# Top-32 attention and capacity routing: which engine makes the product and the mask of a unit, and when a pair is turned

## The chip, the cores and the metric

The kernel runs on one core of a Trainium2 chip. A core has five engines that work side by side, each with its own queue of instructions in order: TensorE (PE in the profile, its weight loads PEld), VectorE (DVE), ScalarE (ACT), GpSimd (POOL) and SyncE (SP), which issues the DMA here. The metric is the device time of one execution in microseconds (us), the median of several runs.

## The reference

Attention of 8 batches x 8 heads over 576 tokens, head dimension 64, in which every row keeps only its 32 largest scores; its output goes into a routed layer with 8 experts of 80 tokens each.

```python
scores = scale * np.matmul(q, k.transpose(0, 1, 3, 2))       # q, k, v: (8, 8, 576, 64), float32
kth = np.partition(scores, -32, axis=-1)[..., -32:-31]
scores = np.where(scores >= kth, scores, -1000000000.0)
attn = np.exp(scores - np.max(scores, axis=-1, keepdims=True))
attn = attn / (np.sum(attn, axis=-1, keepdims=True) + 1e-09)
x = np.matmul(attn, v)                  # then (B,H,S,D) -> (4608, 512)
# ... gate: softmax of x @ w_gate, the best expert of each token
# ... each expert keeps its 80 tokens of highest gate weight:
#     out = gate_w * (relu(x @ w1) @ w2), zero for all other tokens
```

The change touches the attention only.

## The kernel before

Two heads of one batch make a head pair (32 of them). A pair's 576 rows are cut into four tiles of 128 rows and a tail of 64. A **unit** is one tile of one head, 128 rows of 576 scores; the tails of both heads make one unit together. So a pair has 9 units, and there are 288.

A unit's way: TensorE multiplies q and k (`front`), ScalarE copies the scores to SBUF (`s`). VectorE finds candidates for the largest (`parts`, six pieces of 96), and `search` takes the 24th largest of them as a guess. ScalarE compares all scores with the guess and counts (`sign`, with an accumulated `cnt`). The **product** `y` of scores and signs leaves the scores below the guess with their order, so that one more maximum gives the eight next ones; the **pick** takes out of these, by the count, the exact 32nd largest, `thr`. The **mask** marks what lies below it.

```python
        def search(self, i):
            # ... three maxima of the candidates, with two match_replace between; after the third:
                    sign = self.rows.tile([P, S], BF16, name="sign", tag="sign")
                    cnt = self.small.tile([P, 1], F32, name="cnt", tag="cnt")
                    nc.scalar.activation(sign, s, Act.Sign, bias=w9[:, 7:8], scale=-1.0, accum_out=cnt)
                yield
            # ...
            y = self.rows.tile([P, S], F32, name="y", tag="y", bufs=1)
            engine = nc.gpsimd if i in self.odd else nc.vector
            engine.tensor_tensor(out=y, in0=s, in1=sign, op=Alu.mult)
            yield
            nc.vector.max(out=w9[:, 8:], in_=y)
            yield
            pick = self.small.tile([P, TOP_K - G0 + 1], F32, name="pick", tag="pick")
            nc.vector.scalar_tensor_tensor(out=pick, in0=past, scalar=cnt, in1=w9[:, 7:], accum_out=self.thr[:, i : i + 1],
                                           op0=Alu.is_equal, op1=Alu.mult)
            yield
```

The product is made by GpSimd for the units in `odd`, by VectorE for the others. The mask is made by ScalarE for the units in `odd`, by GpSimd for the others:

```python
        def below(self, i):

            self.top.pop(i)
            mask = self.mask_of(i)
            if i in self.odd:
                nc.scalar.activation(mask, self.s[i], Act.Relu, bias=self.thr[:, i : i + 1], scale=-1.0)
                return
            nc.gpsimd.tensor_scalar(mask, self.s[i], self.thr[:, i : i + 1], None, op0=Alu.is_lt)
```

`turn_w` **turns** the scores of a whole tile (both heads) on TensorE and adds the turned mask, times a very large negative number, into the same PSUM. ScalarE takes the exponential out of PSUM (`wT`). `back` multiplies with v, `over` takes the reciprocal of the row sums, `divide` scales the output, and `norm` stores it, turns it (`xT`) and multiplies with the gate's weights (logits).

```python
        def turn_w(self, n, t, between=None):
            # ...
            for c, o in enumerate(dst):
                nc.tensor.matmul(o, lhsT=sc[:, keys[c]], rhs=ident, start=c in (0, NF, NF + 1), stop=False, is_transpose=True,
                                 skip_group_check=True)
            if between:
                between()

            for c in sorted(range(len(dst)), key=lambda c: c != NF):
                nc.tensor.matmul(dst[c], lhsT=mk[:, keys[c]], rhs=minus if self.lean else huge, start=False, stop=True,
                                 skip_group_check=True)
            # ... two exponentials on ScalarE
```

`front`, `turn` (q and k of the next pair), the turn in `norm` and the logits share one PSUM tile with a single buffer, `self.ps_s`.

A whole tile's or the tail's last unit is `whole`. `run` writes out the instructions in steps. Step i works on several units at different stages; the schedule is manual, so each engine gets its instructions in this order. The letters: `G` one of the six candidate maxima of unit i, `a` the first maximum of its candidates, `b c d e` the rest of the search for unit i-1 (`e` ends with ScalarE's sign), `y` the product, `g` the maximum over it, `h` the pick, `m` the mask, `z` the reciprocals.

```python
            self.odd = set(range(1, NU, 2))
                # ...
                lag = dict(a=0, b=1, c=1, d=1, e=1, y=2, g=3, h=4, m=4)

                for c in "ghmGbGycGdGGGeaz" if i % 2 else "GbGhmgcGdGeGGyaz":
                    if c == "G":
                        if 0 <= i < NU:
                            next(first[i])
                    elif c == "a":
                        if 0 <= i < NU:
                            next(first[i], None)
                            second[i] = self.search(i)
                            next(second[i])
                    elif c == "z":
                        for u in drawn:
                            self.over(*u)
                    elif c == "m":
                        if 0 <= i - lag[c] < NU:
                            self.below(i - lag[c])
                    elif i - lag[c] in second:
                        next(second[i - lag[c]])
                done = list(drawn)
                # ...
                def back():
                    if whole(i - 5):
                        self.back(*units[i - 5][:2])
                        drawn.append(units[i - 5][:2])
                # ...
                rest = whole(i - 4) and units[i - 4][2] == 2
                if rest:
                    back()
                def gate():
                    for g in later:
                        if ready[g] == 2:
                            ready[g] = next(g)

                if whole(i - 4):
                    self.turn_w(*units[i - 4][:2], gate)
                for u in done:
                    self.divide(*u)
                # ...
                f = i + 4 if i not in (0, 1) else i + 3
                busy = 0 <= f < NU and units[f][2] != 1
                if busy:
                    self.front(*units[f][:2])
                if not rest:
                    back()
                if due and not busy and i > 0:
                    self.turn(due.pop())
                    busy = True
                for g in list(later):
                    if (ready[g] == 1 and busy or ready[g] == 2 and i < NU + 4) and not last:
                        continue
                    busy = busy or ready[g] == 1
                    ready[g] = next(g, None)
                # ... the next stage of norm
```

Of the kernel before, what the change touches and what calls it, by code (L numbers as in the profile page):

```python
# [9 lines left out]
F32 = mybir.dt.float32  # L10
# [17 lines left out]
def kernel(  # L28
# [12 lines left out]
    B, H, S, D = q.shape  # L41
# [8 lines left out]
    P = 128  # L50
# [13 lines left out]
    NU = NP * UPP  # L64
# [84 lines left out]
    class Attention:  # L149


        def __init__(self, stack, lean):
            self.lean = lean
            pool = lambda name, bufs, **kw: stack.enter_context(tc.tile_pool(name=name, bufs=bufs, **kw))
            self.nat, self.qkp, self.rows = pool("nat", 1), pool("qkp", 2), pool("rows", 2)
            self.small, vpool = pool("small", 4), pool("vpool", 1)
            self.ps_s, self.ps_w, self.ps_c = (pool(n, k, space=PSUM) for n, k in (("ps_s", 1), ("ps_w", 1), ("ps_c", 2)))
            self.qk, self.turned, self.lg = {}, {}, {}
            self.s, self.top, self.cnt, self.y, self.mask, self.w, self.xn = ({} for _ in range(7))
            self.both_s = {}  # L160
            self.thr, self.z = thr_all, z_all
            self.odd = set()


            self.vb = []
            for j in range(1 if lean else 3):
                t = vpool.tile([P, 3 * NF + 4, D + 1], F32, name=f"vb{j}")
                nc.gpsimd.memset(t[:, :, D : D + 1], 1.0)
                nc.gpsimd.memset(t[TL:, 3 * NF, :], 0.0)
                nc.gpsimd.memset(t[:TL, 3 * NF + 1 :, :], 0.0)  # L170
                self.vb.append(t)

            self.xT = vpool.tile([P, NK * P], F32, name="xT")
            nc.gpsimd.memset(self.xT[:, S:], 0.0)
# [49 lines left out]
        def front(self, n, t):  # L224

            qT, kT = self.turned[n]
            m = P if t < NF else TL
            i = n * UPP + 2 * t
            ps = self.four()
            for j in range(2):  # L230
                for h in range(2):
                    d = slice(D * h, D * h + D)
                    o = ps[:, 2 * h + j, :HS] if t < NF else ps[TL * h : TL * h + TL, j, :HS]
                    nc.tensor.matmul(o, lhsT=qT[d, t * P : t * P + m], rhs=kT[d, j * HS : (j + 1) * HS], start=True, stop=True)  # L234
            g = 2 if t < NF else 1
            s = self.rows.tile([P, 2 * S], F32, name="s", tag="s", bufs=2 if self.lean else 5)
            self.both_s[n, t] = s
            for h in range(g):
                self.s[i + h] = s[:, h * S : (h + 1) * S]
            for j in range(0, 2 * g, 2 if i == 0 else 2 * g):  # L240
                w = 2 if i == 0 else 2 * g
                nc.scalar.activation(s[:, j * HS : (j + w) * HS].rearrange("p (j c) -> p j c", c=HS), ps[:, j : j + w, :HS],  # L242
                                     Act.Copy, scale=TINY)
# [205 lines left out]
        def run(self, slow):  # L449

            units = []
            for n in range(NP):
                for t in range(NF):
                    units += [(n, t, 0), (n, t, 1)]
                units.append((n, NF, 2))
            self.odd = set(range(1, NU, 2))
            first, second = {}, {}
            later = []
            due = []
            drawn = []  # L460
            ready = {}

            def whole(i):

                return 0 <= i < NU and units[i][2] > 0

            def step(i, last):
                if 0 <= i < NU:
                    n, t, h = units[i]
                    if t == 2 and h == 1 and n + 2 < NP:  # L470
                        self.load(n + 2, *divmod(n + 2, HP))
                    if t == 3 and h == 1 and n + 2 < NP:
                        self.load_v(n + 2, *divmod(n + 2, HP))
                    if t in (1, 3) and h == 0 and slow and n:
                        slow.pop(0)()
                    if t == 0 and h == 0 and n + 1 < NP:
                        due.append(n + 1)
                    first[i] = self.parts(i)

                lag = dict(a=0, b=1, c=1, d=1, e=1, y=2, g=3, h=4, m=4)  # L480

                for c in "ghmGbGycGdGGGeaz" if i % 2 else "GbGhmgcGdGeGGyaz":
                    if c == "G":
                        if 0 <= i < NU:
                            next(first[i])
# [6 lines that stand above are left out]
                        for u in drawn:  # L492
                            self.over(*u)
                    elif c == "m":
                        if 0 <= i - lag[c] < NU:
                            self.below(i - lag[c])
                    elif i - lag[c] in second:
                        next(second[i - lag[c]])
                done = list(drawn)
                drawn.clear()  # L500

                def back():
                    if whole(i - 5):
                        self.back(*units[i - 5][:2])
                        drawn.append(units[i - 5][:2])


                rest = whole(i - 4) and units[i - 4][2] == 2
                if rest:
                    back()  # L510
                def gate():
                    for g in later:
                        if ready[g] == 2:
                            ready[g] = next(g)

                if whole(i - 4):
                    self.turn_w(*units[i - 4][:2], gate)
                for u in done:
                    self.divide(*u)

                ends = [(n, range(NK) if n < NP - 1 else range(NF) if t < NF else range(NF, NK))
                        for n, t in done if t == NF or (n == NP - 1 and t == NF - 1)]
# [8 lines that stand above are left out]
                    self.turn(due.pop())  # L531
                    busy = True
                for g in list(later):
                    if (ready[g] == 1 and busy or ready[g] == 2 and i < NU + 4) and not last:
                        continue
                    busy = busy or ready[g] == 1
                    ready[g] = next(g, None)
                    if ready[g] is None:
                        later.remove(g)
                for n, cs in ends:  # L540
                    b, hp = divmod(n, HP)
                    later.append(self.norm(n, b, hp, b % 2, 2, cs))
                    ready[later[-1]] = 0

            with tc.manual_schedule():
                for n in range(2):
                    self.load(n, *divmod(n, HP))
                    self.load_v(n, *divmod(n, HP))
                nc.sync.dma_start(wg, moe_w_gate.rearrange("(c p) e -> p c e", p=P))
                self.turn(0)  # L550
                i = -4
                while i < NU + 6 or later:
                    step(i, i >= NU + 5)
                    i += 1
            assert not slow and not due

# [389 lines left out]
```

## Time and profile before

989.52 us, median of 3 runs (988.08 to 991.57). The profiled execution has a span of 986.1 us.

| engine | busy us | share of the span |
|---|---|---|
| TensorE | 865.1 | 88% |
| VectorE | 866.3 | 88% |
| ScalarE | 786.7 | 80% |
| GpSimd | 451.9 | 46% |

The attention takes the span up to about 860 us; routing and experts follow. Shares of the whole span mix both, so the stretches of the attention are to be read by themselves. A row of the groups names the line of the kernel, the engine, the operation, what is written and read, the shape, the count, the busy time in us, the mean duration in ns of one, and behind the bar the time that the engine sat idle before these instructions, with what ended most of it. Instructions of one engine overlap a little at their ends, so busy time is less than the sum of the durations. In the list of waits each line gives the engine that waited, for what, the total in us, the number of times and the longest.

### The profile page before, as it was taken

The page shows a single profiled execution, that of the slowest core. Times are in us where ns is not written, and L with a number is a line of the kernel's source. Part 1 is how long each engine was busy: PE and PEld are TensorE (multiplying, and loading weights), DVE is VectorE, ACT ScalarE, POOL GpSimd, SP SyncE. Part 2 cuts the span into 40 slices and gives each one's busy share as a digit, 9 for nine tenths or more (in the row PEclk, how much of TensorE's full clock was granted, in tenths as well). Part 3 has the DMA queues.
Part 4 walks back from the last instruction along what each step waited for, and adds up shares of the span by engine and source line. Part 5 has one row for each costly group of instructions (what it writes and reads, how often), then busy time and mean ns, then how long its engine had stood idle before and what let it go on. Part 6 is the DMA issues. An engine that isn't in the chain of part 4 may idle for free.

```text
span 986.1 us, 35265 instructions
## 1 busy us (share of the span) xinstructions
PE 865.1 (88%) x13112; PEld 679.3 (69%) x13112; DVE 866.3 (88%) x5072; ACT 786.7 (80%) x1652; POOL 451.9 (46%) x333
## 2 busy tenths in 40 slices
PE   5898989898898998998889898988898898699896
PEld 3676767676666776776667676666676776578896
DVE  5999999999999999999999999999999999561110
ACT  4899999999899999999999999998999998501110
POOL 2455545555455555454555555554555555201111
PEclk9999999999999999999999999999999999979999
DMA  3445453333333333332221222222222200085910
GB/s 86 111 131 139 133 141 100 100 99 99 80 95 99 88 93 99 99 99 68 57 57 48 52 50 53 57 57 57 57 57 56 55 17 14 17 338 180 375 52 25
DMA packets 189812, 90.99 MB, mean 92 GB/s; under 512 B 139712, under 2 KB 176576, under 8 KB 189632
## 3 DMA queue, kind: packets, MB, share of 16 engines
q1 hardware_dynamic: 188608, 86.03, 31.5%
q0 software_dynamic: 1024, 2.62, 0.9%
q8 instruction: 105, 1.72, 0.7%
q14 instruction: 75, 0.61, 0.2%
HBM read 68.44 MB, written 20.19 MB: 90 GB/s over the span
## 4 chain that ended last, share of the span: by engine, by line
DVE 59%; PE 29%; ACT 7%; issue 3%; POOL 1%; DMA 1%; SPq 0%; POOLq 0%; ACTq 0%; DVEq 0%
DVE cand L250 19%; DVE w L275 14%; DVE cand L269 7%; DVE y L273 7%; PE cc L357 6%; PE sp L234 4%; DVE top L261 4%; PE yp L830 4%; PE sp L209 4%; DVE pick L278 3%; DVE w L261 2%; PE ab L334 2%; ACT wT L344 2%; ACT mask L294 1%; PE ab L340 1%
## 5 line engine op out<-in xcount | busy, mean ns | idle before, releaser
L250 DVE MAX8 cand<-s 128x8 f32<-128x96 f32 x1728 | 389.6, 246 | 9.1 <-ACT s L242 8.9
L296 POOL TENSOR_SCALAR mask<-s,thr_all 128x576 bf16<-128x576 f32 x144 | 247.9, 1722 | 149.6 <-DVE pick L278 130.1
L273 POOL TENSOR_TENSOR y<-s,sign 128x576 f32<-128x576 f32 x144 | 184.5, 1281 | 261.8 <-DVE pick L278 121.9
L266 ACT ACTIVATE sign<-s,w 128x576 bf16<-128x576 f32 x288 | 224.9, 781 | 29.6 <-DVE w L261 27.3
L357 PEld LDWEIGHTS cc<-vb,wT 128*64 128x64 f32 x5760 | 182.1, 138 | 92.0 <-ACT wT L344 90.7
L357 PE MATMUL cc<-vb,wT 128*64 128x65 f32 x5760 | 204.4, 225 | 25.7 <-ACT wT L344 25.7
L275 DVE MAX8 w<-y 128x8 f32<-128x576 f32 x288 | 216.6, 752 | 1.3 <-POOL y L273 1.3
L234 PE MATMUL sp<-both 64*128 64x288 f32 (+1 forms) x1280 | 202.0, 435 | 5.7 <-ACT s L242 3.8
L242 ACT ACTIVATE s<-sp 128x1152 f32<-128x1152 f32 (+1 forms) x161 | 167.6, 1042 | 10.5 <-PE sp L234 9.8
L334 PE MATMUL ab<-ident,s 128*128 128x128 f32 x1148 | 175.9, 281 | 0.0
L344 ACT ACTIVATE wT<-ab 128x1024 f32<-128x1024 f32 (+1 forms) x159 | 149.6, 941 | 5.6 <-PE ab L340 4.1
L234 PEld LDWEIGHTS sp<-both 64*128 64x128 f32 (+1 forms) x1280 | 105.5, 179 | 45.2 <-ACT s L242 6.2
L334 PEld LDWEIGHTS ab<-ident,s 128*128 128x128 f32 x1148 | 127.2, 141 | 11.7 <-issue 0.9
L340 PEld LDWEIGHTS <-mask 128*128 128x128 bf16 x1312 | 76.9, 97 | 79.1 <-issue 37.3
L261 DVE MAX8 top<-cand 128x8 f32<-128x48 f32 x576 | 115.2, 200 | 0.0
L294 ACT ACTIVATE mask<-s,thr_all 128x576 bf16<-128x576 f32 x144 | 113.0, 785 | 0.5
L269 DVE MATCH_REPLACE8 cand<-top,cand 128x48 f32<-128x48 f32 x576 | 111.0, 193 | 0.1
L273 DVE TENSOR_TENSOR y<-s,sign 128x576 f32<-128x576 f32 x144 | 106.6, 740 | 0.8 <-ACT sign L266 0.8
L340 PE MATMUL ab<-huge,mask 128*128 128x128 bf16 x1148 | 89.9, 219 | 0.0
L340 PE MATMUL cc<-huge,mask 128*128 128x128 bf16 x160 | 35.7, 223 | 58.9 <-ACT mask L294 29.0
L380 ACT ACTIVATE xn<-cc,z_all 128x64 f32<-128x64 f32 (+1 forms) x320 | 85.8, 315 | 1.2 <-DVE z_all L369 0.8
L278 DVE SCALAR_TENSOR_TENSOR pick<-past,cnt,w 128x9 f32<-128x9 f32 x288 | 66.4, 230 | 0.2 <-DVE z_all L369 0.2
(187 smaller groups left out, 856.0 us busy)
## 6 DMA issues: line engine op xcount, KB each, us to landing
w<-in_moe_w_dram SPq DMA_DIRECT2D x10, 2048.0 KB, 16.0
vb<-in_v_dram SPq DMA_DIRECT2D x96, 128.0 KB, 2.7
w<-in_moe_w_dram SPq DMA_DIRECT2D x24, 512.0 KB, 3.8
out_dram<-zero SPq DMA_DIRECT2D x9, 1024.0 KB, 5.8
qn<-in_q_dram SPq DMA_DIRECT2D x64, 128.0 KB, 2.3
kn<-in_k_dram SPq DMA_DIRECT2D x64, 128.0 KB, 2.6
xd<-xn SPq DMA_DIRECT2D x32, 256.0 KB, 2.2
qn<-in_q_dram SPq DMA_DIRECT2D x32, 32.0 KB, 2.5
```

What stands on the lines that cost most here:

```text
L234: nc.tensor.matmul(o, lhsT=qT[d, t * P : t * P + m], rhs=kT[d, j * HS : (j + 1) * HS], start=True, stop=True)
L250: nc.vector.max(out=cand[:, j, :], in_=s[:, j * S // NG : (j + 1) * S // NG])
L261: nc.vector.max(out=dst, in_=cand)
L266: nc.scalar.activation(sign, s, Act.Sign, bias=w9[:, 7:8], scale=-1.0, accum_out=cnt)
L269: nc.vector.match_replace(out=cand, in_to_replace=dst, in_values=cand, imm_value=LOW)
L273: engine.tensor_tensor(out=y, in0=s, in1=sign, op=Alu.mult)
L275: nc.vector.max(out=w9[:, 8:], in_=y)
L296: nc.gpsimd.tensor_scalar(mask, self.s[i], self.thr[:, i : i + 1], None, op0=Alu.is_lt)
L334: nc.tensor.matmul(o, lhsT=sc[:, keys[c]], rhs=ident, start=c in (0, NF, NF + 1), stop=False, is_transpose=True, skip_group_check=True)
L340: nc.tensor.matmul(dst[c], lhsT=mk[:, keys[c]], rhs=minus if self.lean else huge, start=False, stop=True, skip_group_check=True)
L344: nc.scalar.activation(wT[:, : g * NF, :], ab.rearrange("p h c r -> p (h c) r")[:, : g * NF, :], Act.Exp, scale=scale / TINY)
L357: nc.tensor.matmul(cc[r : r + TL, o], lhsT=wT[:, h * NF + c if c < NF else 2 * NF, r : r + TL], rhs=vb[:, k, :], start=(c == 0), stop=(c = ...
```

## The change

The pattern of who makes what goes from every second unit to two of three: of three successive units, two have GpSimd's product and ScalarE's mask, one has VectorE's product and GpSimd's mask. So 192 instead of 144 products are GpSimd's and 96 instead of 144 VectorE's; 192 instead of 144 masks are ScalarE's and 96 instead of 144 GpSimd's. It is meant to take work from VectorE.

VectorE and GpSimd are to be kept out of each other's way: in the step in which VectorE makes a product, the maximum over GpSimd's last product, the pick and the masks stand late, just before VectorE's product; GpSimd's mask comes one step later than before (5 steps behind its unit). So that masks are there before they are needed, a tile is turned 6 instead of 4 steps behind its second unit, and multiplied with v 7 instead of 5 behind. The scores live two steps longer, and get 7 instead of 5 buffers; the small tiles get 5 instead of 4.

```diff
@@ class Attention @@
-            self.small, vpool = pool("small", 4), pool("vpool", 1)
+            self.small, vpool = pool("small", 5), pool("vpool", 1)
 ...
-            s = self.rows.tile([P, 2 * S], F32, name="s", tag="s", bufs=2 if self.lean else 5)
+            s = self.rows.tile([P, 2 * S], F32, name="s", tag="s", bufs=2 if self.lean else 7)
@@ run @@
-            self.odd = set(range(1, NU, 2))
+            self.odd = set(i for i in range(NU) if i % 3 < 2)
 ...
-                lag = dict(a=0, b=1, c=1, d=1, e=1, y=2, g=3, h=4, m=4)
-
-                for c in "ghmGbGycGdGGGeaz" if i % 2 else "GbGhmgcGdGeGGyaz":
+                lag = dict(a=0, b=1, c=1, d=1, e=1, y=2, g=3, h=4)
+
+                for c in "GbGcGdGeGghmGyaz" if i % 3 == 1 else "ghmGbGycGdGGGeaz":
 ...
-                        if 0 <= i - lag[c] < NU:
-                            self.below(i - lag[c])
+
+                        for k in (4, 5):
+                            if 0 <= i - k < NU and (i - k in self.odd) == (k == 4):
+                                self.below(i - k)
 ...
                 def back():
-                    if whole(i - 5):
-                        self.back(*units[i - 5][:2])
-                        drawn.append(units[i - 5][:2])
+                    if whole(i - 7):
+                        self.back(*units[i - 7][:2])
+                        drawn.append(units[i - 7][:2])
 ...
-                rest = whole(i - 4) and units[i - 4][2] == 2
+                rest = whole(i - 6) and units[i - 6][2] == 2
 ...
-                if whole(i - 4):
-                    self.turn_w(*units[i - 4][:2], gate)
+                if whole(i - 6):
+                    self.turn_w(*units[i - 6][:2], gate)
 ... the ends of the loops over the steps are moved by 2 as well
```

More of the change, by code (lines that the diff above doesn't have):

```diff
@@ L533, in step @@
                 for g in list(later):
-                    if (ready[g] == 1 and busy or ready[g] == 2 and i < NU + 4) and not last:
+                    if (ready[g] == 1 and busy or ready[g] == 2 and i < NU + 6) and not last:
                         continue
@@ L551, in run @@
                 i = -4
-                while i < NU + 6 or later:
-                    step(i, i >= NU + 5)
+                while i < NU + 8 or later:
+                    step(i, i >= NU + 7)
                     i += 1
```

## The prediction, made before the changed kernel was run

> **What bounds the kernel now.** I read the page first (engines, slices, groups), then stretches of 100 us, the list of waits, and last the order of time over one cycle of nine units (one head pair). In the stretches (columns: span, then PE, PE weight load, DVE, ACT, POOL busy, granted clock, DMA share, GB/s):
> ```profile
> 300.00:400.00 100.00, 89.69 (x1292) 68.87 (x1292) 99.80 (x599) 93.08 (x197) 52.35 (x35) 1.00 0.35 93
> ...
> 500.00:600.00 100.00, 90.41 (x1305) 69.69 (x1301) 99.91 (x601) 93.35 (x196) 52.32 (x35) 1.00 0.23 55
> ...
> 94.11:770.23 676.12, 606.31 (x8764) 466.90 (x8766) 675.25 (x4046) 627.60 (x1318) 351.29 (x235) 1.00 0.31 79
> ```
> VectorE has no idle time from 100 to 800 us: it is the bound. But ScalarE stands at 93% and TensorE at 90%. GpSimd issues one instruction per unit (a product or a mask), so 94.11 to 770.23 holds 234 units, 26 cycles: 676.12 / 26 = 26.00 us per cycle, and 288 units are 32 cycles. ScalarE's busy time is 627.60 / 26 = 24.14 us of each 26.00.
>
> The groups that the change touches (busy us, mean ns, then the engine's idle time before them):
> ```profile
> L296 POOL TENSOR_SCALAR mask<-s,thr_all 128x576 bf16<-128x576 f32 x144 | 247.9, 1722 | 149.6 <-DVE pick L278 130.1
> L273 POOL TENSOR_TENSOR y<-s,sign 128x576 f32<-128x576 f32 x144 | 184.5, 1281 | 261.8 <-DVE pick L278 121.9
> ...
> L294 ACT ACTIVATE mask<-s,thr_all 128x576 bf16<-128x576 f32 x144 | 113.0, 785 | 0.5
> ...
> L273 DVE TENSOR_TENSOR y<-s,sign 128x576 f32<-128x576 f32 x144 | 106.6, 740 | 0.8 <-ACT sign L266 0.8
> ```
> GpSimd, at 46% of the span, has room; ScalarE has not. The waits that bear on it:
> ```profile
> PEld L340 <- POOL mask L296: 31.1, 21, 1.9
> PE cc L340 <- ACT mask L294: 29.0, 40, 0.8
> ACT sign L266 <- DVE w L261: 27.3, 53, 1.3
> ...
> ACT both L222 <- PE sp L209: 21.7, 31, 2.1
> ```
> TensorE waits for masks of both engines, without cost while VectorE is full. ScalarE's idle time is of two kinds: 27.3 us waiting for VectorE, which goes away when VectorE is no longer the bound, and waits for TensorE, which need not.
>
> **What the Trainium skill says.** "SBUF — State Buffer", section "Who interferes with whom": a VectorE instruction with two SBUF inputs and a GpSimd instruction that reads SBUF exclude one another; whoever comes second waits for the whole of the first. The trace agrees once, near the end:
> ```profile
> 845.85 1.28 POOL L273 TENSOR_TENSOR y<-s,sign 128x576 f32<-128x576 f32 x1 [1.04 <-DVE pick L278]
> 845.87 1.29 DVE L278 SCALAR_TENSOR_TENSOR pick<-past,cnt,w 128x9 f32<-128x9 f32 x1
> ```
> A pick of 213 ns (median) took 1.29 us, just the length of GpSimd's product. In the middle there is hardly a collision: VectorE's products have a mean of 740 ns and a maximum of 759. One that started at 504.95 still took 0.74 us though a GpSimd mask was recorded until 505.22, so the lock's last quarter microsecond is not seen here. "ScalarE: Activation LUTs", section "What ACT_TABLE_LOAD costs", gives an ACTIVATE with a pointer bias 280 ns + 0.833 ns per element, and an overlap of about 93 ns with the next: my estimate for 576 elements is 760 and 667 net; the trace has 785, and 0.67 from a mask's start to the next start (514.54 to 515.21).
>
> **The change part by part.**
>
> *VectorE.* 48 of its 144 products go to GpSimd. From such a product's start to the next instruction's start is 0.66 us (821.94 to 822.60), so 1.5 per cycle free 0.99 us: 26.00 - 0.99 = 25.01 us. If nothing else mattered, 32 x 0.99 = 32 us.
>
> *GpSimd.* 48 products more, 48 masks fewer: 48 x (1.281 - 1.722) = -21 us. It does not bind.
>
> *ScalarE.* 48 masks more, 1.5 x 0.67 = 1.0 us per cycle. The sum of one cycle after, by start-to-next-start times read between 505.82 and 525.99: 9 signs x 0.765 = 6.89; 6 masks x 0.67 = 4.02; exponentials 4 x (0.19 + 0.92) + 0.72 = 5.16; divisions 4 x 0.39 + 0.64 = 2.20; copies of scores 4 x 1.01 + 0.53 = 4.57; turned q and k 1.02; the x turn 0.54; gate part 0.08. Together 24.48 us, half a microsecond under VectorE's 25.01. That is without any wait for TensorE.
>
> *Order.* The new string gives VectorE's product and the pick of that step a place after GpSimd's product and mask. Counting along it, a sign has some 1.5 to 2 us until its product is needed, about as before. A late GpSimd mask can still hold the pick.
>
> *Turn two steps later.* This takes away TensorE's waits for masks (58.9 us in the group of the first mask matmul). But it also puts other work side by side. By position in the cycle, the turns stood at steps 5, 7, 0, 2, 3 and the score matmuls at 5, 7, 0, 2, 4; now both stand at 0, 2, 4, 5, 7. The short tail unit's turn falls at step 5, straight after step 4 with its turn, its gate logits (moved there from step 0) and its scores. And the PSUM tile for scores has one buffer, shared by scores, q/k turns, x turn and logits, so ScalarE and TensorE hand it to and fro.
>
> With ScalarE as the late engine and its signs always ready, I laid that handover out by the trace. From a score copy's end to ScalarE's next use of the same tile:
> 1. x turn, step 3: TensorE needs 1.08 us from the sign's start (505.82 to 506.90) and ScalarE has only a sign of 0.77: idle 0.31.
> 2. q/k turn, step 1: 1.87 us (511.65 to 513.52) against a sign and a mask, 1.45: idle 0.42.
> 3. step 4: the logits between transposes and mask matmuls put the exponentials some 0.1 us late.
> 4. step 5: exponential, value product, tail turn and scores in a row. The same links in the trace:
> ```profile
> 516.16 1.03 ACT L344 ACTIVATE wT<-ab 128x1024 f32<-128x1024 f32 x1
> ...
> 517.24 1.39 PE L357 MATMUL cc<-vb,wT 128*64 128x65 f32 x40
> ...
> 518.55 0.66 PE L334 MATMUL ab<-ident,s 128*128 128x128 f32 x4
> ...
> 519.53 1.19 PE L234 MATMUL sp<-both 64*64 64x288 f32 x8
> ```
> That is 1.08 + 1.31 + 0.98, then 1.24 for full scores and 0.05 to the copy: 4.66 us. Meanwhile ScalarE has 0.92 + 0.39 + 0.53 + 0.67 + 0.77 + 0.72 = 4.00: idle 0.66.
>
> The four gaps are 1.49 us; 24.48 + 1.49 = 25.97 us per cycle, against 26.00 now. So the place of VectorE's bound would be taken by the ScalarE-TensorE handover at nearly the same length.
>
> *The end.* With the turn later, one more pair is unturned when VectorE has finished. At the end pairs follow one another by 4.25 us (846.65 to 850.90). Less the blocked pick (1.29 - 0.21), some 3 us are added.
>
> Sum: 989.5 - 32 x 0.03 + 3 = 992 us.
>
> **The rivals.**
>
> A. *Handover as bound*, as above: 992. For it: ScalarE's 93%, and the wait for the q/k turn already seen in all 31 of them. Against it: gaps 3 and 4 are laid out by hand, and TensorE, which no longer waits for masks, might come earlier to the tail.
>
> B. *Only the unavoidable gaps remain* (1 and 2): 24.48 + 0.73 = 25.21 us, 32 x 0.79 = 25 us saved, 3 given back: 967. For it: the string and the lag look fitted to each other. With VectorE alone as the bound (25.01) it would be 961; I hold that for unlikely, as ScalarE would need 98% occupancy.
>
> C. *The port collides.* In the step before VectorE's product, GpSimd's product is followed at once by its mask (1.28 + 1.72 = 3.0 us). If signs come late from a full ScalarE, the mask runs into the pick, 0.2 to 0.8 us per cycle. By itself VectorE would be at 25.0 + 0.8 = 25.8, still hidden behind A; in series with A's gaps, 32 x 0.5 = 16 us more: about 1008.
>
> **Range and chances.** I weigh A three to one against B: 0.75 x 992 + 0.25 x 967 = 986 us. An error of 0.3 us per cycle in the hand-laid gaps is 10 us; that, and a part of C above, gives 971 to 1002. Over 2% faster means below 969.7, so B or better: 0.17. Over 2% slower means above 1009.3, so C in full: 0.08. Within 2%: 0.75.
>
> **What would show it.** Right: VectorE falls from 99.9% to 96-97% in the middle stretches and its idle time is put down to ScalarE's sign; ScalarE rises to 96% or more, with its idle time before the q/k copy, the x copy and the score copy after the tail turn; TensorE's waits for masks are nearly gone; nine units take about 25.8 us. Wrong towards B: nine units take 25.2 us, and the score copies don't wait. Wrong towards C: picks or VectorE's products with means well over 230 and 740 ns. Wrong altogether if VectorE stays above 99% with a cycle near 25.0.

## The result: slower by 1.5%, and what the profile after shows

The changed kernel takes 1005.16 us against 990.02 us (medians of four runs each): ratio 1.0153, 95% interval 1.0126 to 1.0179. The prediction was 986 us with a range of 971 to 1002, so the result lies outside it, beyond rival A (992). Rival C's figure, 1008, is nearest, but by luck: the collisions of picks and products that it was made of did not come (below).

The stretches of the changed kernel (columns as before: span, PE, PE weight load, DVE, ACT and POOL busy, clock, DMA share, GB/s):

```profile
69.68:810.12 740.44, 651.02 (x9437) 509.86 (x9438) 708.65 (x4312) 696.06 (x1460) 357.65 (x253) 0.99 0.31 79
500.00:600.00 100.00, 89.04 (x1297) 69.79 (x1297) 95.86 (x587) 95.15 (x200) 48.12 (x34) 1.00 0.22 53
```

The first runs from the third to the thirty-first copy of the turned q and k on ScalarE (the q/k copy, one per head pair): 28 cycles of nine units. In the kernel before the same stretch is 727.70 us:

```profile
71.25:798.95 727.70, 652.92 (x9437) 502.83 (x9438) 726.83 (x4354) 675.80 (x1417) 378.33 (x253) 1.00 0.31 80
```

VectorE is no longer full: 96 instead of 99.9%. ScalarE went from 93 to 94%. No engine is saturated.

The groups of the changed kernel that answer to those shown before (busy us and mean ns of one; then the idle us just before them and what ended most of it):

```profile
L273 POOL TENSOR_TENSOR y<-s,sign 128x576 f32<-128x576 f32 x192 | 245.6, 1279 | 445.8 <-DVE pick L278 168.1
...
L296 POOL TENSOR_SCALAR mask<-s,thr_all 128x576 bf16<-128x576 f32 x96 | 165.3, 1722 | 3.1 <-DVE pick L278 3.1
...
L294 ACT ACTIVATE mask<-s,thr_all 128x576 bf16<-128x576 f32 x192 | 149.2, 778 | 0.8
...
L273 DVE TENSOR_TENSOR y<-s,sign 128x576 f32<-128x576 f32 x96 | 72.1, 751 | 28.5 <-ACT sign L266 28.5
...
L278 DVE SCALAR_TENSOR_TENSOR pick<-past,cnt,w 128x9 f32<-128x9 f32 x288 | 61.2, 212 | 0.0
```

The counts are as meant and the mean durations are near those of before (VectorE's product 751 ns against 740, the picks 212 against 230): the products and picks do not collide. But VectorE now sits idle for 28.5 us in front of its own products, waiting for ScalarE's sign. The list of waits of the changed kernel says what ScalarE in turn waits for (who waits, for whom: us in total, times, longest):

```profile
DVE y L273 <- ACT sign L266: 28.5, 58, 0.8
ACT s L242 <- PE sp L234: 27.4, 36, 2.4
...
ACT both L222 <- PE sp L209: 15.7, 31, 2.1
```

ScalarE waits for TensorE, once per cycle in the score copy, once in the q/k copy, and more shortly in the copy of the turned x. The waits of TensorE for masks, which stood in this list before the change (27.8 us for GpSimd's and 24.3 us for ScalarE's between 100 and 800 us), are gone. What stands at the score copy is the chain laid out in the prediction, in order of time (start in us, length in us, engine, line, operation; in brackets the idle time before it and what ended it):

```profile
499.77 0.64 ACT L397 COPY xT<-sp 128x576 f32<-128x576 f32 x1 [0.20 <-PE sp L209]
...
502.20 1.02 ACT L344 ACTIVATE wT<-ab 128x1024 f32<-128x1024 f32 x1
...
503.28 1.39 PE L357 MATMUL cc<-vb,wT 128*64 128x65 f32 x40
...
503.51 0.66 ACT L242 ACTIVATE s<-sp 128x576 f32<-128x576 f32 x1
...
504.60 0.66 PE L334 MATMUL ab<-ident,s 128*128 128x128 f32 x4
...
505.57 1.24 PE L234 MATMUL sp<-both 64*128 64x288 f32 x8
...
506.86 1.13 ACT L242 ACTIVATE s<-sp 128x1152 f32<-128x1152 f32 x1 [0.58 <-PE sp L234]
...
519.86 1.12 ACT L222 COPY both<-sp 128x1152 f32<-128x1152 f32 x1 [0.32 <-PE sp L209]
```

From the exponential (502.20) to the score copy (506.86) it is 4.66 us, as laid out, and ScalarE is idle for 0.58 us before the copy. This longest link is TensorE's own queue rather than the score tile: ScalarE had done with the tile by 504.17, but the scores of 505.57 stand behind the value product and the tail's turn, which follow one another without a pause. Before the x copy and the q/k copy ScalarE is idle for 0.20 and 0.32 us; there TensorE fills the one score tile again only after ScalarE's score copy. No run gives the tile a second buffer, so what the single buffer costs by itself is not shown.

The starts of the q/k copies, one per cycle, divide the loss. Three of the 28 cycles hold the gates of two batches (the softmax of the logits and the choice of the expert, mostly VectorE's work); the other 25 are called plain.

| | before | after | difference |
|---|---|---|---|
| start to the third q/k copy | 71.25 us | 69.68 us | -1.6 us |
| 25 plain cycles | 25.84 us each | 26.09 us each | +6.3 us |
| 3 cycles with gates | 27.23 us each | 29.36 us each | +6.4 us |
| thirty-first copy to the first turn of the routing (861.02, 878.70) | 62.07 us | 68.58 us | +6.5 us |

Together 17.7 us (from unrounded times), nearly the whole difference of the spans, 1004.1 - 986.1 = 18.0.

The granted clock of TensorE (the third figure from the end of a stretch) differs too. In the kernel before it was 1.00 all through the stretch above. In the changed kernel it was about 0.5 for 3.4 us in each of the three cycles with gates and once at the end, as here; a value product then took 2.37 us instead of 1.39:

```profile
489.30:492.70 3.40, 3.40 (x45) 2.95 (x45) 3.40 (x18) 2.75 (x6) 0.88 (x1) 0.51 0.00 0
...
857.86 2.37 PE L357 MATMUL cc<-vb,wT 128*64 128x65 f32 x40 [1.90 <-ACT wT L344]
```

In each of the three cycles it sets in about when TensorE takes up work again after an idle time of 2.82 us, in which it waited for an exponential. What brings the slow clock about is not shown.

### The profile page after: what moved, and what is told of

Read it like the earlier page. It is cut to its first block, busy times and chain, and to the rows that moved or that the text cites. A ratio compares the mean times of both kernels' runs of the same rounds, so it can differ in the third digit from the quotient of the medians.

```text
span 1004.1 us, 35154 instructions
## 1 busy us (share of the span) xinstructions
PE 865.3 (86%) x13112; PEld 689.6 (69%) x13112; DVE 843.1 (84%) x5024; ACT 810.1 (81%) x1700; POOL 428.4 (43%) x333
## 4 chain that ended last, share of the span: by engine, by line
DVE 45%; PE 25%; ACT 23%; issue 4%; POOL 2%; DMA 1%; POOLq 0%; SPq 0%; DVEq 0%; ACTq 0%
DVE cand L250 14%; DVE w L275 10%; ACT sign L266 9%; PE cc L357 5%; DVE cand L269 5%; PE sp L209 5%; DVE y L273 4%; ACT wT L344 4%; PE yp L832 4%; ACT s L242 4%; DVE top L261 3%; ACT mask L294 2%; DVE pick L278 2%; ACT xn L380 2%; PE sp L234 2%
## 5 line engine op out<-in xcount | busy, mean ns | idle before, releaser
L273 POOL TENSOR_TENSOR y<-s,sign 128x576 f32<-128x576 f32 x192 | 245.6, 1279 | 445.8 <-DVE pick L278 168.1
L250 DVE MAX8 cand<-s 128x8 f32<-128x96 f32 x1728 | 395.4, 247 | 8.8 <-ACT s L242 8.8
L357 PEld LDWEIGHTS cc<-vb,wT 128*64 128x64 f32 x5760 | 184.5, 139 | 140.7 <-ACT wT L344 128.7
L357 PE MATMUL cc<-vb,wT 128*64 128x65 f32 x5760 | 206.9, 226 | 70.4 <-ACT wT L344 68.6
L242 ACT ACTIVATE s<-sp 128x1152 f32<-128x1152 f32 (+1 forms) x161 | 166.9, 1038 | 28.2 <-PE sp L234 27.4
L296 POOL TENSOR_SCALAR mask<-s,thr_all 128x576 bf16<-128x576 f32 x96 | 165.3, 1722 | 3.1 <-DVE pick L278 3.1
L294 ACT ACTIVATE mask<-s,thr_all 128x576 bf16<-128x576 f32 x192 | 149.2, 778 | 0.8
L273 DVE TENSOR_TENSOR y<-s,sign 128x576 f32<-128x576 f32 x96 | 72.1, 751 | 28.5 <-ACT sign L266 28.5
L340 PEld LDWEIGHTS <-mask 128*128 128x128 bf16 x1312 | 84.6, 98 | 2.2
L334 PE MATMUL cc<-ident,s 128*128 128x128 f32 x160 | 45.6, 285 | 33.0 <-ACT xn L380 33.0
L278 DVE SCALAR_TENSOR_TENSOR pick<-past,cnt,w 128x9 f32<-128x9 f32 x288 | 61.2, 212 | 0.0
```

The lines of the kernel that those rows point to most:

```text
L250: nc.vector.max(out=cand[:, j, :], in_=s[:, j * S // NG : (j + 1) * S // NG])
L357: nc.tensor.matmul(cc[r : r + TL, o], lhsT=wT[:, h * NF + c if c < NF else 2 * NF, r : r + TL], rhs=vb[:, k, :], start=(c == 0), stop=(c = ...
```

## The experiments

Theory H: in the changed kernel the plain cycle is a chain handed to and fro between ScalarE and TensorE, in part through the one score tile, with VectorE's own 25.0 us below it. Rivals: VectorE and GpSimd shutting each other out, the port of the prediction (P), the later turn by its places alone (L), ScalarE's masks wherever the turn stands (M). A cycle below always means the distance of two q/k copies, read from the trace; times are medians, ratios to the kernel before on the same chip.

**1. The later turn alone.**

```diff
 # kernel before, with
-                if whole(i - 4):
-                    self.turn_w(*units[i - 4][:2], gate)
+                if whole(i - 6):
+                    self.turn_w(*units[i - 6][:2], gate)
 # likewise back at i - 7; score buffers 7, small buffers 5
```

> The kernel before with the later turn alone (turn 6, value product 7 steps behind, 7 score buffers); products and masks alternate as before. Theory H (the new bound is the handover of the one score tile between ScalarE and TensorE, and ScalarE's extra masks are what made it the longer one): ScalarE here has 1.0 us less per cycle of nine units than in the changed kernel, 26.1 - 1.0 = 25.1, so VectorE stays the bound; plain cycles 25.8 us as before, and only the end grows, by about 6 us: 994 to 996 us. Rival L (the later turn alone, which puts turns and score matmuls into the same steps, makes the cycle): 26.1 us per plain cycle, about 1002 us.

1014.6 us, ratio 1.0245 (1.0228 to 1.0262): slower than the whole change. The cycles are irregular, 25.9 to 27.9 us, with a mean of 26.55 without the gate cycles; the four longest contain 3.4 us of the slow clock each, and without them the mean is 26.34. H's number is missed and L is nearer. ScalarE's waits in the stretch from 100 to 800 us:

```profile
ACT both L222 <- PE sp L209: 19.7, 26, 1.7
ACT s L242 <- PE sp L234: 17.0, 30, 0.7
```

The expectation took the gaps as fixed and subtracted a mask. They are not fixed: with fewer masks ScalarE comes to the handover earlier and waits longer there (19.7 us for the q/k turn against 12.3 in the changed kernel over the same stretch).

**2. The two-of-three pattern alone.**

```diff
 # kernel before, with
-            self.odd = set(range(1, NU, 2))
+            self.odd = set(i for i in range(NU) if i % 3 < 2)
-                for c in "ghmGbGycGdGGGeaz" if i % 2 else "GbGhmgcGdGeGGyaz":
+                for c in "GbGhmgcGdGeGGyaz" if i % 3 == 1 else "ghmGbGycGdGGGeaz":
```

> The kernel before with two of three units for GpSimd's product and ScalarE's mask, and nothing else: pick, masks and turn stand where they stood. If VectorE and GpSimd shut each other out (theory P for what the late pick is for), GpSimd's mask goes ahead of its product in the step before VectorE's, the product ends about 1.4 us into that step, and pick and maximum wait about 0.7 us three times per cycle: 25.0 + 2.1 = 27.1 us per plain cycle, about 1030 us, with picks up to 1 us long. If that is no matter, about 26.1 us per cycle as in the changed kernel, 995 to 1000 us, and picks of 0.21 us.

1039.17 us, ratio 1.0498 (1.048 to 1.0515), 27.4 us per plain cycle: P, and a little more than laid out. In order of time:

```profile
564.25 1.72 POOL L296 TENSOR_SCALAR mask<-s,thr_all 128x576 bf16<-128x576 f32 x1 [1.35 <-DVE cand L250]
565.94 1.28 POOL L273 TENSOR_TENSOR y<-s,sign 128x576 f32<-128x576 f32 x1
...
566.24 1.00 DVE L278 SCALAR_TENSOR_TENSOR pick<-past,cnt,w 128x9 f32<-128x9 f32 x1
```

GpSimd's product follows its mask, the pick comes 0.3 us after the product's start and ends with it: 1.00 us for what takes 0.21. Such an instruction counts as busy: VectorE shows 99.98% from 500 to 600 us in this kernel, though it does less than before. So the late pick of the change does what it is for; the collision it avoids is worth more than the products that the pattern takes from VectorE.

**3. Without the turn of x, the logits and the gates** (x is still stored; nothing is routed, so the time after the attention isn't comparable).

```diff
             yield 1
+            return
             ps = self.four()[:, :2, :].rearrange("p j c -> p (j c)")
```

> The changed kernel without the turn of x, the gate logits and the gates (x is stored, but nothing is routed). Theory H: ScalarE loses 0.62 us of work and the two gaps at the x turn and the logits, 26.1 - 0.62 - 0.3 - 0.1 = 25.0 to 25.1 us per plain cycle, where VectorE with 25.0 becomes the bound again; no cycle with gates; attention shorter by some 32 x 1.0 + 10 us: about 960 us. Rival (port collisions or VectorE's order hold the cycle): 26.1 us per cycle stay, only the three gate cycles go: about 993 us.

954.85 us, ratio 0.9658 (0.9642 to 0.9674). All cycles take 25.00 to 25.02 us (one 25.13), and VectorE is nearly full again, as the stretch from 500 to 600 us of this run shows (columns as before, VectorE the third after the length), with what it still waits for between 100 and 800 us:

```profile
500.00:600.00 100.00, 85.81 (x1252) 67.65 (x1248) 98.82 (x609) 96.13 (x202) 51.04 (x37) 1.00 0.23 56
...
DVE y L273 <- ACT sign L266: 8.3, 28, 0.4
```

Only ScalarE's and TensorE's work got less in a plain cycle (and one addition of VectorE's, 0.18 us), and the cycle is 1.08 us shorter. So H holds for the changed kernel. But VectorE is still idle before its product for ScalarE's sign in every cycle, 8.3 / 28 = 0.30 us, and ScalarE waited for VectorE only once: the chain is shortened here and is still the bound. VectorE's own bound lies below 25.01 us here, and the run does not show where.

**4. The gates one step later.**

```diff
                 yield 0
+                yield 0
                 yield from self.gates(b - bi, nb)
```

> The changed kernel with the gates of each second batch begun one step later, so that their subtraction (two SBUF inputs) no longer stands beside a GpSimd product. If the collision (1.18 instead of 0.24 us) is what makes the cycle with gates 29.4 us: 28.4 us there, plain cycles 26.1 as before, 3 us less in all, about 1002 us. If the gates cost because VectorE has to do them on top of everything: 29.4 stays, 1005 us.

997.42 us, ratio 1.0077 (1.006 to 1.0094): 8 us less than the changed kernel, more than the 3 expected. Plain cycles stay at 26.09; those with gates take 27.08, 27.09 and 28.12 instead of 29.41, 29.45 and 29.23, together 5.8 us less, and the end is 1.6 us shorter. The pair in the changed kernel, in order of time:

```profile
476.21 1.27 POOL L273 TENSOR_TENSOR y<-s,sign 128x576 f32<-128x576 f32 x1 [3.02 <-DVE top L261]
...
476.40 1.18 DVE L425 TENSOR_TENSOR lg<-lg,mx 128x80 f32<-128x80 f32 x1
```

and one step later, with GpSimd idle, the same subtraction in the run with the gates later (one line further down in its source):

```profile
478.15 0.24 DVE L426 TENSOR_TENSOR lg<-lg,mx 128x80 f32<-128x80 f32 x1
```

The subtraction has two SBUF inputs and waited for GpSimd's product, 0.94 us too long. That is less than half of the 2.3 us that two of the cycles gained. In these two the slow clock is gone as well; the third, which gained 1.1 us, still has it:

```profile
697.40:700.80 3.40, 3.40 (x14) 2.50 (x15) 3.40 (x23) 2.04 (x4) 1.27 (x1) 0.50 0.30 69
```

So the 3.3 us that a cycle with gates takes above a plain one in the changed kernel can be split, as an estimate from different runs: 1.0 for the gates without either (27.08 - 26.09), 1.0 for the slow clock (28.12 - 27.08) and 1.1 to 1.3 for the collision (29.23 to 29.41, less 28.12). Run 7 agrees: two of its cycles with gates have the collision (1.18 and 1.19 us) without the slow clock, and take 27.70 us, 2.0 above its plain ones. The end is shorter for the same reason: the exponentials that follow one another across the logits are 4.9 us apart at full clock, 6.5 in the changed kernel.

**5. and 6. The late pick with the turn at 4, and at 5, steps.**

```diff
 # changed kernel, 4 steps: turn_w at i - 4, back at i - 5, masks all 4 steps behind,
 # GpSimd's issued behind its product:
-                for c in "GbGcGdGeGghmGyaz" if i % 3 == 1 else "ghmGbGycGdGGGeaz":
+                for c in "GbGcGdGeGghmGyaz" if i % 3 == 1 else {0: "ghGbGymcGdGGGeaz", 2: "ghmGbGycGdGGGeaz"}[i % 3]:
 # changed kernel, 5 steps: only turn_w at i - 5, back at i - 6
```

> The changed kernel with the turn back at 4 steps (and the value product at 5); GpSimd's mask is issued one step earlier, behind GpSimd's product, so that it still comes before its turn. Pattern and late pick stay. Theory L (since the later turn alone cost 25 us: the places of the turns in the cycle make the handover between ScalarE and TensorE long): with the places of the kernel before only the gap at the q/k turn (0.42) and small ones (0.25) are left, 24.5 + 0.7 = 25.2 us per plain cycle, up to 25.5 if TensorE waits for GpSimd's mask; 25 x 0.7 + some 3 us at the end less than the changed kernel, about 983 us. Rival M (ScalarE's masks themselves, wherever the turn stands): 26.1 us, 1002 us.

> The changed kernel with the turn 5 steps behind instead of 6 (value product 6), nothing else. The turns then stand at steps 6, 8, 1, 3, 4 of the cycle, all but one away from the score matmuls. If it is only turns and scores in the same step that cost: 25.2 us per plain cycle, about 983 us. If it is every chain through the one score tile: the logits and the q/k turn now share step 1, and the tail's turn follows the value product in step 4; laid out by hand gaps of 0.8, 0.7 and 0.2 us, 24.5 + 1.7 = 26.2 us, 1004 us.

1092.04 us, ratio 1.105 (1.1031 to 1.1068), and 1102.41 us, ratio 1.1152 (1.113 to 1.1174). The numbers expected are missed by 90 to 119 us. With the turn at 4, in order of time:

```profile
507.64 1.72 POOL L296 TENSOR_SCALAR mask<-s,thr_all 128x576 bf16<-128x576 f32 x1
...
509.42 0.23 PE L340 MATMUL cc<-huge,mask 128*128 128x128 bf16 x1 [1.78 <-POOL mask L296]
...
511.87 2.30 PE L357 MATMUL cc<-vb,wT 128*64 128x65 f32 x40
...
514.28 0.17 DVE L369 RECIPROCAL z_all<-cc 128x2 f32<-128x2 f32 x1 [2.15 <-PE cc L357]
```

The mask comes late, TensorE waits for it, the value product ends late (with 2.30 us it also falls into a stretch of the slow clock), and VectorE stands 2.15 us in front of the reciprocal, which is in its queue in order. I read this as a loop through all four engines, which the expectation had not followed. At 5 steps VectorE waits the same way for TensorE (107.9 us), and TensorE waits for ScalarE's copy of x before it may refill the score tile; the waits of that run from 100 to 800 us:

```profile
DVE z_all L369 <- PE cc L357: 107.9, 68, 3.0
PEld sp L234 <- ACT xT L397: 63.8, 23, 3.2
```

The slow clock adds to both, and is the smaller part: the plain cycles with it take about 29.7 us (14 of 25) and 30.1 us (18 of 25), those without it 28.3 and 28.6, still over 2 us above the changed kernel's.

So the later turn isn't a fault by itself: the late pick needs it, and at 6 steps it is the best of the three places. The weight of the two lists of events is a reading of the traces; no run takes the reciprocal's wait away alone.

**7. ScalarE's sign without its count.** The pick compares with a constant, so each row keeps its 24 largest scores: part of the search is left out.

```diff
-                    nc.scalar.activation(sign, s, Act.Sign, bias=w9[:, 7:8], scale=-1.0, accum_out=cnt)
+                    nc.scalar.activation(sign, s, Act.Sign, bias=w9[:, 7:8], scale=-1.0)
-            nc.vector.scalar_tensor_tensor(out=pick, in0=past, scalar=cnt, in1=w9[:, 7:], accum_out=self.thr[:, i : i + 1],
+            nc.vector.scalar_tensor_tensor(out=pick, in0=past, scalar=past[:, 0:1], in1=w9[:, 7:], accum_out=self.thr[:, i : i + 1],
```

> The changed kernel with ScalarE's sign without its accumulated count; the pick compares with a constant, so the 24th largest score is taken as the bound of every row (part of the search is left out, the number of instructions on the other engines is the same). Only ScalarE gets shorter, by about 0.09 us per sign or 0.8 us per cycle. Theory H (ScalarE, with its four waits for TensorE, sets the plain cycle): 26.1 - 0.8 = 25.3 us, VectorE's 25.0 being near; some 25 us less than the changed kernel, 980 us. Rival (a loop through VectorE, GpSimd and the port, in which the sign's 0.1 us are a small part): 25.9 us or more, 998 us and up.

992.74 us, ratio 1.0045 (1.0032 to 1.0058): 12 us less than the changed kernel. Plain cycles take 25.71 us, 0.38 less, between the two expectations. From a sign's start to the next start is 0.66 instead of 0.77 us, so nine signs give about 0.9 us, but less than half of it arrives. That fits a chain in two engines: the signs of steps 1, 3 and 5, and that of step 4 beside the logits, lie in stretches in which ScalarE waits for TensorE anyway, and there a shorter sign makes a longer wait. These stretches keep their length to 0.01 us in the trace: 1.09 us from the sign to the x copy, 2.43 (2.42 here) on to the exponential behind the logits, 4.66 from there to the score copy, 1.87 from the sign to the q/k copy. Five of nine signs times 0.1 would be 0.5. H stands, but ScalarE's sum plus fixed gaps, as in the prediction, isn't the way to subtract.

**8. to 10. ScalarE keeps one mask of three; GpSimd takes the rest.** GpSimd had half its time free.

```diff
 # changed kernel, with
-            if i in self.odd:
+            if i in self.odd and i % 3 == 0:        # ScalarE's mask
-                for c in "GbGcGdGeGghmGyaz" if i % 3 == 1 else "ghmGbGycGdGGGeaz":
 # run 8: GpSimd's masks 5 and 6 steps behind; H is a pick 5 steps behind
+                for c in ("gGbGymcGdGGGeaz", "GbGcGdGeGghHmGyaz", "ghGbGymcGdGGGeaz")[i % 3]:
 # run 9: all masks 4 steps behind
+                for c in ("GbGcGdhgGyGGemaz", "GbGcGdGeGghmGyaz", "ghGbGymcGdGGGeaz")[i % 3]:
 # run 10: run 9 with the gates one step later
```

> The changed kernel with ScalarE's mask for one unit of three only; GpSimd, which makes the product of two of three, also makes the masks of two of three, each behind a product, and the pick of the unit with VectorE's product is moved to the step of that product, so that picks and VectorE's products meet a free port. Turn 6 behind as in the changed kernel. Theory H: ScalarE has 3 x 0.67 = 2.0 us less per cycle, 22.5 + 1.5 to 2 = 24.5 us at most, so VectorE is the bound again with 25.0 to 25.3 us; about 980 us. Rival L (as the kernel before with the later turn alone, which had 1.0 us less of ScalarE's work and was slower yet): 26 us or more, 1000 us and up.

> As the run in which ScalarE keeps one mask of three, in another order: both GpSimd masks are issued 4 steps behind, straight behind a GpSimd product, so that each is ready before the step of its turn begins; in the step before VectorE's product the pick stands after five candidate maxima, where GpSimd's mask is nearly done. If the 26.1 us of the first such run came from GpSimd's mask arriving in the step of its turn (1.04 us of TensorE's wait, then the exponentials, the score copy, the next sign, VectorE's product): 25.2 to 25.5 us per plain cycle, about 980 us. If the places of the turns alone make 26.1 us whatever ScalarE has to do: 26.1 us, 1003 us.

> The same with the gates begun one step later. With VectorE as the bound the gates cost their own VectorE time, 1.4 us each as in the kernel before, unless they meet a GpSimd instruction: within 3 us of the run without it, about 977 us.

Run 8: 1003.35 us, ratio 1.0147 (1.013 to 1.0165), 26.13 us per plain cycle, although ScalarE is at 89%. Its chain in order of time:

```profile
520.75 1.73 POOL L296 TENSOR_SCALAR mask<-s,thr_all 128x576 bf16<-128x576 f32 x1
...
522.53 0.23 PE L340 MATMUL cc<-huge,mask 128*128 128x128 bf16 x1 [1.04 <-POOL mask L296]
...
523.25 1.02 ACT L344 ACTIVATE wT<-ab 128x1024 f32<-128x1024 f32 x1 [0.17 <-PE ab L340]
...
526.49 0.76 DVE L273 TENSOR_TENSOR y<-s,sign 128x576 f32<-128x576 f32 x1 [0.45 <-ACT sign L266]
```

A mask that GpSimd makes in the step of its turn holds TensorE by 1.04 us, and through the exponential, the score copy and the next sign in ScalarE's queue VectorE's product. Run 9 only changes when products, masks, maxima and picks are issued (which of these counts is not told apart): 981.74 us, ratio 0.9923 (0.9897 to 0.9949), 25.32 us per plain cycle, as expected. So with the turns at the same places as in the change the cycle can be 25.3 us, and L, the places alone, is out. M is not told apart from H: ScalarE's masks are links of the same chain. Run 10: 977.09 us, ratio 0.9887 (0.9867 to 0.9908), the fastest version: 1.1% less than the kernel before and 28 us less than the changed kernel. Its cycles with gates take 26.71 us, the ones behind them 25.99, and up to 830 us it has no stretch of the slow clock, where run 9 has two. From 500 to 600 us VectorE is at 99% and GpSimd at 70:

```profile
500.00:600.00 100.00, 91.61 (x1344) 71.99 (x1346) 98.65 (x604) 91.14 (x194) 70.30 (x48) 1.00 0.24 56
```

## Why the prediction was wrong, point by point

- *VectorE, 25.01 us.* Right as a sum: VectorE is busy for 24.90 us of a plain cycle of the changed kernel, and the plain cycle before less the 0.99 us saved is 25.84 - 0.99 = 24.85. That run 3 took 25.01 us, too, is chance: the forecast figure contained the gates, and run 3 has none and is bound by the chain.
- *Rival A's 25.97 us for the handover.* Right for the plain cycle, 26.09 measured; the gaps, laid out as 0.31, 0.42, 0.1 and 0.66, were 0.20, 0.32, 0.10 and 0.58 us of idle time in the trace. The prediction counted ScalarE's work from start to start; a recorded instruction ends some 0.1 us after the start of its successor (a mask takes 0.78 us, the next instruction starts after 0.67), so idle times come out about that much shorter. The signs named for A came true: VectorE at 96%, idle before its product for ScalarE's sign, ScalarE idle before the q/k and score copies, masks no longer waited for.
- *"25.97 us per cycle, against 26.00 now".* This step failed first. The 26.00 is a mean that contains the gates; a plain cycle before took 25.84. Setting them against each other assumed that the gates would disappear beside the handover. Plain cycles gave +6.3 instead of -1 us: of the 0.28 us missed in each, 0.16 are this comparison (26.00 - 25.84) and 0.12 the handover itself (26.09 - 25.97).
- *The gates.* They were not in the sum at all. Above a plain cycle they cost 1.4 us before and 3.3 after; the three cycles are 6.4 us longer. A collision with GpSimd's product is part of it, of the kind rival C feared for the picks (these stayed at 212 ns), and the slow clock is another (run 4).
- *The end, +3 us.* +6.5. From the last sign to the routing there are three exponentials before and four after; the two that follow one another across the logits are 6.5 us apart (856.79 and 863.27) where I had set 4.25 for every pair. About 1.6 us of that is the slow clock: the same two are 4.9 us apart in run 4. The start gave back 1.6, which the sum had left out.
- *The weights.* A alone said 992; a quarter of B, which kept only two of four gaps, took that to 986. All four gaps were there. With the four parts as measured the sum is 989.5 + 6.3 + 6.4 + 6.5 - 1.6 = 1007 us, within 2 us of the result; that shows that no large part is missing, not why each is as long as it is.
- *"The later turn takes away TensorE's waits".* Right, and run 5 shows that with the turn at 4 steps the late pick costs 100 us. What the prediction lacked is the measure of it: alone it costs 25 us (run 1).

## What to carry to other kernels

When a full engine is relieved, the next bound may be no engine but a chain that two others hand to and fro, in part through a single buffer: lay it out link by link, and count work that lies beside its waits as free and the rest as full price. Set plain cycles against plain cycles, and put the rare stage (here the gates) into the sum by itself, since what hid beside the old bound need not hide beside the new. Look at the granted clock of the stretches that grew before giving all of their growth to one cause. Work moved to an idle engine is better placed by when its result is needed than by how busy that engine is: the same masks on GpSimd gave 1003 or 982 us by the order of issue alone.

## What the runs showed of the hardware that was not expected

- A VectorE instruction blocked by GpSimd counts as busy: with the pattern alone VectorE showed 99.98% while picks took up to 1.09 us instead of 0.21. The mean and the maximum of a duration show it, the busy share doesn't.
- GpSimd's mask, with one input, takes 1722 ns for 576 elements, longer than its product with two inputs, 1281 ns.
- The count that ScalarE accumulates beside the sign costs 0.1 us net (0.77 to 0.66 us from start to start), though its own instruction shows 0.20.
- TensorE's granted clock was about 0.5 for single stretches of 3.4 us, four times between 40 us and the last exponential in the changed kernel, once in the kernel before. Where VectorE was full it cost nothing: of the cycles with gates in the run with the pattern alone, the one with such a stretch took 29.32 us, the two without it 29.33 and 29.32. With the turn at 4 steps a plain cycle took 29.7 us with it and 28.3 without.
